# Turning a second x chunk on TensorE at the start of a gated attention and MLP kernel, and assigning the last tile's PSUM banks anew

## The chip, the cores and the metric

The kernel runs on one core of one Trainium2 chip. The metric is the device time of the program in microseconds (us). A "look" below is one profiled execution: its span (first to last instruction) is some 1.7 us shorter than the device time of the same run. All runs quoted here were fast: none lies more than 1.5% above the fastest of its kernel. Ratios are computed as the mean time of one kernel's fast runs over that of the other's fast runs of the same rounds, so they are not quite the ratio of the medians that are quoted.

Engines: PE is TensorE (PEld its weight loads), DVE is VectorE, ACT is ScalarE, POOL is GpSimd, SPq is the queue of SyncE, from which most DMAs are issued. A DMA "lands" at the last of its 16 landing records. "Granted clock" is the share of TensorE's full clock that the trace's clock records show; in these traces products of 128 columns follow each other by 107 ns at half clock and by 56 at full clock.

## The reference, cut to what matters

```python
def reference(A_x, A_wqkv, A_wo, B_x, B_w1, B_w2, B_w3, B_w4, gate_w):
    x = A_x                                                # 1 x 2048 x 640, bf16
    g = sigmoid((x * gate_w).sum(-1, keepdims=True))
    a = linear_attention(x, A_wqkv, A_wo)                  # needs q, k, v = x @ wqkv
    b = mixer_and_mlp(x, B_w1, B_w2, B_w3, B_w4)           # ends in x1 + gelu(ln(x1) @ w3) @ w4
    return g * a + (1 - g) * b
```

The kernel cuts the 2048 rows into 16 chunks of 128. Its first work is k = x @ wk for each chunk, with the gate as an extra, 641st column. For that, x must be transposed. Its last work is the product with W4, for four tiles of 512 rows each.

## The kernel before: the parts that matter

The head. Loads are issued on SPq and ACT's queue; chunk 0 of x is loaded plainly and transposed ("turned") on PE, chunks 1 to 15 are transposed by DMA. "Fillers" are products of constants that keep PE busy, meant to bring its full clock early (the clock records have it at 4.06 us here; the one look without fillers, below, at 7.58).

```python
    load_x(0, 1)                                           # SPq
    aq.dma_start(g5[:], gate_w...)                         # ACT's queue
    load_wk(sp, 1); load_wk(aq, 0); load_wk(aq, 2); load_wk(sp, 3); load_wk(aq, 4)   # 160 KB each
    for c0, c1 in ((1, 2), (2, 3), (3, 4), (4, 6), (6, 8), (8, 12), (12, 16)):
        load_xT(c0, c1)                                    # DMA transposes, SPq
    ...
    warmup(6)                                              # six fillers of 512 columns
    warmup(3, P)                                           # three of 128
    ... # turn x chunk 0 (bf16 transposes, two PSUM pairs), DVE copies it to xT;
    ... # the gate (5 rows) is transposed between the two groups
    warmup(3, P)
    for dc in range(DC):                                   # K of chunk 0, weight piece by piece
        k_mm(kp, 0, (dc,))
        if dc < DC - 1:
            warmup(1, 2 * P)
    k_evac(kp, 0)
    for c in range(1, NCH):
        pt = pair(); k_mm(pt, c, range(DC)); k_evac(pt, c)
```

The tail. A PSUM "pair" is two banks, and the kernel has four pairs. For the last tile, row blocks 1 and 3 are computed in the order wide group (512 columns), wide group, narrow group (128), narrow group; wide and narrow group of one block share one pair.

```python
    def w4_dst(t, cc, pts, hf):
        n = D - TS if t == NT - 1 and cc % 2 else LT
        return (pts[cc][:, 0, TS - n:TS], 0, n) if hf == 0 else (pts[cc][:, 1, 0:D - n], n, D)
    ...
        for cc, hf in ((1, 1), (3, 1), (1, 0), (3, 0)) if last else ((1, 0), (1, 1), (3, 0), (3, 1)):
            ...
            w4_mm(t, cc, pts, hf, False)
            if last:
                w4_part(t, cc, pts, hf)                    # DVE reads the group, DMA stores it
```

## Time and profile before

| what | before |
|---|---|
| device time | 265.14 us median of 3 runs; 265.31 of 4 with the run taken beside the changed kernel |
| span of the look | 263.5 us, PE busy 98% |
| turn of chunk 0 starts | 3.66 us |
| K of chunk 0 / 1 / 8 starts | 4.72 / 6.92 / 16.79 us |
| last product starts | 260.56 us |

The page's busy shares, and the engine line of the chain that ended last:

```profile
PE 258.4 (98%) x1722; PEld 161.0 (61%) x1740; DVE 141.4 (54%) x276; ACT 82.7 (31%) x123; POOL 20.2 (8%) x65
PE 92%; SPq 3%; DMA 3%; issue 1%; DVE 0%
```

With PE in 92% of the chain, only the places where PE waits can give time back. They are at the two ends. The timeline of PE in the head (start and duration in us, engine, line, operation, out<-in, shape, count, and in brackets the idle time and what ended it):

```profile
3.66 0.42 PE L205 MATMUL pp<-ident,x_sb 128*128 128x128 bf16 x2
4.01 0.18 PE L208 MATMUL pp<-ident,g 5*128 5x5 bf16 x1
...
4.72 0.43 PE L184 MATMUL pp<-wk_sb,xT 128*128 128x320 bf16 x2
...
5.83 0.43 PE L184 MATMUL pp<-wk_sb,xT 128*128 128x320 bf16 x2 [0.19 <-DMA wk_sb<-in_A_wqkv_dram]
...
6.59 0.64 PE L184 MATMUL pp<-wk_sb,xT 128*128 128x320 bf16 x3
```

PE turns x from 3.66 us, starts K at 4.72 and waits for the third weight piece, which landed at 5.79. Two of the three products in the last line end chunk 0; the third begins chunk 1, at 6.92, 0.05 us after the DMA transpose of chunk 1 landed at 6.87. Landings to the hundredth are read from the records in the trace; the view of a tile's instructions gives them as issue to landing, here for the transpose of chunk 1 (issued at 2.18):

```profile
L121 SPq DMA_TRANSPOSE xT<-in_A_x_dram x1: 1305/1305/1305, 2.2 to 2.2; - x1
...
DMA to landing us min/median/max: 4.7/4.7/4.7
```

From then on each chunk takes 1.362 us, until chunk 8 waits for the transpose of chunks 8 to 11 (PE timeline, later window):

```profile
16.79 11.07 PE L184 MATMUL pp<-wk_sb,xT 128*128 128x320 bf16 x80 [0.16 <-DMA xT<-in_A_x_dram]
```

In the tail, PE's weight loads and DVE show the other wait:

```profile
259.09 1.08 DVE L498 SCALAR_TENSOR_TENSOR oc<-pp,omg,x 128x512 bf16<-128x512 f32 x2 [2.05 <-PE pp L470]
259.87 1.66 SPq L500 DMA_DIRECT2D out_dram<-oc  x3
259.89 0.71 PEld L470 LDWEIGHTS <-h 128*128 128x128 bf16 x12 [0.24 <-issue]
260.81 0.35 DVE L498 SCALAR_TENSOR_TENSOR oc<-pp,omg,x 128x128 bf16<-128x128 f32 x1 [0.65 <-PE pp L470]
```

The last narrow group starts at 259.89 us, 336 ns after the product before it, where products of this size follow each other by 56 ns. It waits until DVE has read (259.09 to 259.84) the wide group of the same block, which lies in the other bank of the same pair. The view names no releaser for this gap ("issue"); that it is the read follows from the 0.05 us between the read's end and the start.

### The profile page before, as it was taken

The numbers are of one execution on the slowest core, as the hardware profiler recorded it, in microseconds if no ns is written. First come the engines' busy times: TensorE is split into PE (matmuls) and PEld (weight loads), VectorE is DVE, ScalarE is ACT, GpSimd is POOL, SyncE is SP. The second block draws the span as 40 slices with busy tenths as digits, with TensorE's granted clock in tenths as the row PEclk, the third lists the DMA queues.
The fourth block names the chain that finished last, engine by engine and source line by source line (L and its number), as shares of the span: only waits on it lengthen the run. The fifth ranks groups of instructions, "written<-read, shape, count | busy, mean of one in ns | idle before, by whom it ended". The sixth has DMA issues, their size and how long they took to land.

```text
span 263.5 us, 4244 instructions
## 1 busy us (share of the span) xinstructions
PE 258.4 (98%) x1722; PEld 161.0 (61%) x1740; DVE 141.4 (54%) x276; ACT 82.7 (31%) x123; POOL 20.2 (8%) x65
## 2 busy tenths in 40 slices
PE   8999999999999999999999999999999999999995
PEld 4767555688755644555667555667565577455743
DVE  1678778899947997955403464413356323112132
ACT  1555454321166236622502222412131332142100
POOL 5000050012210041001000001000001000000000
PEclk9999999999999999999999999999999999999999
DMA  7999988016672567700132000051100051100011
GB/s 191 175 193 370 374 261 322 0 27 124 124 99 57 101 111 172 248 0 2 25 75 77 25 0 2 0 100 52 50 0 2 0 101 52 50 0 2 0 50 50
DMA packets 46413, 24.14 MB, mean 92 GB/s; under 512 B 35770, under 2 KB 45626, under 8 KB 46394
## 3 DMA queue, kind: packets, MB, share of 16 engines
q1 hardware_dynamic: 45952, 23.39, 34.7%
q10 hardware_dynamic: 442, 0.49, 0.5%
q8 instruction: 13, 0.21, 0.3%
q14 instruction: 6, 0.05, 0.1%
HBM read 12.21 MB, written 2.62 MB: 56 GB/s over the span
## 4 chain that ended last, share of the span: by engine, by line
PE 92%; SPq 3%; DMA 3%; issue 1%; DVE 0%
PE pp L470 21%; PE pp L450 21%; PE pp L298 8%; PE pp L434 8%; PE pp L403 8%; PE pp L332 8%; PE pp L226 8%; PE pp L184 4%; DMA xT<-in_A_x_dram 3%; SPq L121 3%; PE pp L370 1%; PE pp L458 1%; PE pp L479 1%; PE pp L351 1%; PE pp L241 0%
## 5 line engine op out<-in xcount | busy, mean ns | idle before, releaser
L450 PE MATMUL pp<-lnxT,w_sb 128*128 128x512 bf16 x249 | 59.8, 379 | 0.6
L470 PE MATMUL pp<-w_sb,h 128*128 128x256 bf16 (+3 forms) x415 | 57.8, 299 | 0.3 <-issue 0.2
L452 ACT ACTIVATE h<-pp 128x1024 bf16<-128x1024 f32 (+1 forms) x28 | 26.9, 962 | 82.2 <-PE pp L450 82.2
L470 PEld LDWEIGHTS <-h 128*128 128x128 bf16 x416 | 39.3, 98 | 18.0 <-issue 1.3
L450 PEld LDWEIGHTS <-w_sb 128*128 128x128 bf16 x260 | 25.5, 98 | 26.8
L486 DVE SCALAR_TENSOR_TENSOR oc<-pp,omg,x 128x640 bf16<-128x640 f32 x14 | 12.0, 881 | 41.4 <-ACT h2x L461 21.3
L437 DVE SCALAR_TENSOR_TENSOR x<-pp,gate,x 128x640 f32<-128x640 f32 x16 | 13.9, 867 | 29.4 <-PE pp L434 29.4
L176 ACT ACTIVATE e<-pp 128x640 bf16<-128x640 f32 (+1 forms) x26 | 21.5, 827 | 9.5 <-PE pp L226 9.5
L434 PE MATMUL pp<-m_sb,pqT 128*128 128x320 bf16 x160 | 24.3, 299 | 0.0
L403 PE MATMUL pp<-w_sb,hsT 128*128 128x320 bf16 x160 | 23.9, 299 | 0.0
L406 DVE TENSOR_TENSOR x<-pp,x_sb 128x640 f32<-128x640 f32 x16 | 13.1, 820 | 19.7 <-PE pp L403 19.6
L184 PE MATMUL pp<-wk_sb,xT 128*128 128x320 bf16 (+1 forms) x160 | 22.7, 300 | 0.3 <-DMA wk_sb<-in_A_wqkv_dram 0.2
L298 PE MATMUL pp<-x_sb,pk 128*128 128x320 bf16 (+1 forms) x160 | 22.3, 300 | 0.0
L226 PE MATMUL pp<-xT,hsT 128*128 128x512 bf16 x98 | 21.6, 379 | 0.1
L298 PEld LDWEIGHTS <-pk 128*128 128x128 bf16 x160 | 18.8, 117 | 3.5
L403 PEld LDWEIGHTS <-hsT 128*128 128x128 bf16 x160 | 15.7, 98 | 8.2
L434 PEld LDWEIGHTS <-pqT 128*128 128x128 bf16 x160 | 15.7, 98 | 7.7
L184 PEld LDWEIGHTS <-xT 128*128 128x128 bf16 x160 | 15.4, 98 | 6.9 <-DMA xT<-in_A_x_dram 0.7
L332 PE MATMUL pp<-lnxT,w_sb 128*128 128x512 bf16 x76 | 17.9, 379 | 0.2
L226 PEld LDWEIGHTS <-hsT 128*128 128x128 bf16 x100 | 11.8, 118 | 9.7
L268 POOL TENSOR_SCALAR rstd<-mv 128x4 f32<-128x4 f32 (+1 forms) x11 | 3.4, 312 | 153.6 <-DVE mv L274 153.6
L177 DVE TENSOR_SCALAR e<-e 128x640 bf16<-128x640 bf16 (+1 forms) x26 | 9.5, 367 | 8.9 <-ACT e L176 7.5
(72 smaller groups left out, 195.0 us busy)
## 6 DMA issues: line engine op xcount, KB each, us to landing
out_dram<-oc SPq DMA_DIRECT2D x14, 160.0 KB, 1.8
w_sb<-in_B_w_dram SPq DMA_DIRECT2D x1, 2160.0 KB, 8.8
w_sb<-in_B_w_dram SPq DMA_DIRECT2D x1, 2080.0 KB, 10.0
x_sb<-in_A_x_dram SPq DMA_DIRECT2D x1, 1280.0 KB
x_sb<-in_A_x_dram SPq DMA_DIRECT2D x1, 1120.0 KB, 8.2
wo_sb<-in_A_wo_dram SPq DMA_DIRECT2D x6, 160.0 KB, 7.7
hsT<-in_A_wqkv_dram SPq DMA_DIRECT2D x1, 800.0 KB, 5.6
m_sb<-in_A_wqkv_dram SPq DMA_DIRECT2D x1, 800.0 KB, 12.8
```

Source lines behind the costliest of these rows:

```text
L176: nc.scalar.activation(ev, src, ACT.Exp)
L184: nc.tensor.matmul(pt[:, hf, 0:n], lhsT=xT[:, dc, c * P:(c + 1) * P], rhs=wk_sb[:, dc, hf * HD:hf * HD + n], start=(dc == 0), stop=(dc == ...
L226: nc.tensor.matmul(pt[:, t % 2, :], lhsT=wq_sb[:, dc, :].rearrange("p (m j) -> p j m", j=DC)[:, j], rhs=xT[:, dc, t * TS:(t + 1) * TS], st ...
L298: nc.tensor.matmul(pt[:, hf, 0:HD + hf], lhsT=w, rhs=x_sb[:, c, hf * HD:(hf + 1) * HD + hf], start=(c == 0), stop=(c == NCH - 1))
L332: nc.tensor.matmul(pt[:, i, :], lhsT=w, rhs=lnxT[t][:, dc, :], start=(dc == 0), stop=(dc == DC - 1))
L403: nc.tensor.matmul(pt[:, hf, 0:HD], lhsT=hsT[:, fc, 2 + c * P:2 + (c + 1) * P], rhs=w2_sb[:, fc, hf * HD:(hf + 1) * HD], start=(fc == 0), ...
L406: nc.vector.tensor_tensor(x1[:].rearrange("p (h e) -> p h e", h=2), pt[:, :, 0:HD], x_sb[:, c, 0:D].rearrange("p (h e) -> p h e", h=2), op ...
L434: nc.tensor.matmul(pt[:, hf, 0:HD], lhsT=pqT[:, j, c * P:(c + 1) * P], rhs=m_sb[:, j, hf * HD:(hf + 1) * HD], start=(j == 0), stop=(j == D ...
L437: nc.vector.scalar_tensor_tensor(x1, pt[:, :, 0:HD], gate[:, c:c + 1], x1, op0=ALU.mult, op1=ALU.add)
L450: nc.tensor.matmul(pt[:, k, :], lhsT=w3_sb[:, dc, fc * P:(fc + 1) * P], rhs=lnT[:, dc, :], start=(dc == 0), stop=(dc == DC - 1))
L452: nc.scalar.activation(h2[:, 2 * i * TS:(2 * i + n) * TS], pt[:].rearrange("p h e -> p (h e)")[:, 0:n * TS], ACT.Gelu_apprx_tanh)
L470: nc.tensor.matmul(dst, lhsT=st[t]["h2"][:, fc * TS + cc * P:fc * TS + (cc + 1) * P], rhs=w4_sb[:, fc, a:b], start=start and fc == 0, stop ...
```

## The change

Intent: in the head, start turning earlier, take the K pieces in the order in which they come, and take one transpose off the DMA queue by turning chunk 1 on PE too. In the tail, place the groups so that the last one does not wait for a read of its own pair. The core of the diff:

```diff
+    g5z = const.tile([P, P], BF16)                     # gate, padded with zeros to 128 rows
...
-    for c0, c1 in ((1, 2), (2, 3), (3, 4), (4, 6), (6, 8), (8, 12), (12, 16)):
+    load_x(1, 2)
+    for c0, c1 in ((2, 3), (3, 4), (4, 6), (6, 8), (8, 12), (12, 16)):
         load_xT(c0, c1)
...
-    warmup(6)
-    warmup(3, P)
+    warmup(5)
+    warmup(1, 3 * P)
...
+                if c:
+                    nc.tensor.transpose(dst, src, ident[:])          # chunk 1: bf16
+                else:
+                    nc.tensor.matmul(dst, lhsT=src, rhs=ident[:], start=True, stop=True)   # chunk 0: float32
+            if c == 0 and b == DC:
+                nc.tensor.matmul(pt[:, 1, 0:DC], lhsT=g5z[:], rhs=ident[:, 0:DC], start=True, stop=True)
...
+    turn(0)
+    warmup(1, TS)
+    for n, dc in enumerate((1, 0, 3, 2, 4)):
+        if n == DC - 1:
+            turn(1)
+        if n:
+            warmup(1, 2 * P)
+        k_mm(kp, 0, (dc,), ...)
...
+            homes = {0: (0, 1), 2: (1, 2)} if 0 in ccs else {1: (3, 3), 3: (2, 0)}   # last tile:
+            for cc, (w, n) in homes.items():                                          # pair of the wide,
+                wide, narrow = pts["pairs"][w][:, 0, :], pts["pairs"][n][:, 1, 0:NW]  # pair of the narrow group
```

The narrow group of block 3 thus lies in pair 0, its wide group in pair 2.

More of the change, by code (lines that the diff above doesn't have):

```diff
@@ L132 @@
     load_wk(aq, 4)
-    for c0, c1 in ((1, 2), (2, 3), (3, 4), (4, 6), (6, 8), (8, 12), (12, 16)):
+    load_x(1, 2)
+    for c0, c1 in ((2, 3), (3, 4), (4, 6), (6, 8), (8, 12), (12, 16)):
         load_xT(c0, c1)
     sp.dma_start(wq_sb, wqkv_v[:, :, 0:D])
-    load_x(1, 8)
+    load_x(2, 8)
     load_x(8, 16)
@@ L178, in phi, with k_mm @@
         nc.vector.scalar_tensor_tensor(dst, src, 0.0, ev, op0=ALU.max, op1=ALU.add)
-    def k_mm(pt, c, dcs, hfs=(0, 1), last=DC - 1):
+    def k_mm(pt, c, dcs, first=0, last=DC - 1):
         for dc in dcs:
-            for hf in hfs:
+            for hf in range(2):
                 n = HD + hf
                 nc.tensor.matmul(pt[:, hf, 0:n], lhsT=xT[:, dc, c * P:(c + 1) * P],
-                                 rhs=wk_sb[:, dc, hf * HD:hf * HD + n], start=(dc == 0), stop=(dc == last))
+                                 rhs=wk_sb[:, dc, hf * HD:hf * HD + n], start=(dc == first), stop=(dc == last))
     def k_evac(pt, c):
@@ L189, in k_evac @@
         phi(pk[:, c, :].rearrange("p (h e) -> p h e", h=2), pt[:, :, 0:HD], D)
+    k0_order = (1, 0, 3, 2, 4)
     warm = pair()
@@ L196, in warmup, with turn @@
             nc.tensor.matmul(warm[:, 1, 0:w], lhsT=one[:, 0:P], rhs=one[:, 0:w], start=True, stop=True)
-    warmup(6)
-    warmup(3, P)
+    nc.vector.memset(g5z[:], 0.0)
+    nc.vector.tensor_copy(g5z[0:DC, :], g5[:])
+    warmup(5)
+    warmup(1, 3 * P)
     kp = pair()
-    turns = [(pair()[:, 0, :].bitcast(BF16), a, b) for a, b in ((0, 2), (2, DC))]
-    tg = warm[:, 0, :].bitcast(BF16)
-    for n, (ptb, a, b) in enumerate(turns):
-        for dc in range(a, b):
-            nc.tensor.transpose(ptb[:, (dc - a) * P:(dc - a + 1) * P], x_sb[:, 0, dc * P:(dc + 1) * P], ident[:])
-        nc.vector.tensor_copy(xT[:, a:b, 0:P], ptb[:, 0:(b - a) * P].rearrange("p (c s) -> p c s", c=b - a))
-        if n == 0:
-            nc.tensor.transpose(tg[:, 0:DC], g5[:], ident[0:DC, 0:DC])
-            nc.vector.tensor_copy(wk_sb[:, :, D], tg[:, 0:DC])
-    warmup(3, P)
-    for dc in range(DC):
-        k_mm(kp, 0, (dc,))
-        if dc < DC - 1:
+    turns = [(pair(), a, b) for a, b in ((0, 2), (2, DC))]
+    def turn(c):
+        for pt, a, b in turns:
+            ptb = pt[:, 0, :].bitcast(BF16) if c else pt[:, 0, :]
+            for dc in range(a, b):
+                dst, src = ptb[:, (dc - a) * P:(dc - a + 1) * P], x_sb[:, c, dc * P:(dc + 1) * P]
+                if c:
[4 more added lines that the diff above has]
+                nc.tensor.matmul(pt[:, 1, 0:DC], lhsT=g5z[:], rhs=ident[:, 0:DC], start=True, stop=True)
+            nc.vector.tensor_copy(xT[:, a:b, c * P:(c + 1) * P],
+                                  ptb[:, 0:(b - a) * P].rearrange("p (c s) -> p c s", c=b - a))
+            if c == 0 and b == DC:
+                nc.vector.tensor_copy(wk_sb[:, :, D], pt[:, 1, 0:DC])
+    turn(0)
+    warmup(1, TS)
+    for n, dc in enumerate(k0_order):
+        if n == DC - 1:
+            turn(1)
+        if n:
             warmup(1, 2 * P)
+        k_mm(kp, 0, (dc,), first=k0_order[0], last=k0_order[-1])
     k_evac(kp, 0)
@@ L461, in w3_rest, with w4_tiles @@
         nc.scalar.activation(st[t]["h2x"][:], dst, ACT.Gelu_apprx_tanh)
-    def w4_dst(t, cc, pts, hf):
-        n = D - TS if t == NT - 1 and cc % 2 else LT
-        return (pts[cc][:, 0, TS - n:TS], 0, n) if hf == 0 else (pts[cc][:, 1, 0:D - n], n, D)
+    NW = D - TS
+    def w4_tiles(t, ccs, pts):
+        if t < NT - 1:
+            for cc in ccs:
+                pt = pair()
+                pts[cc, 0], pts[cc, 1] = (pt[:, 0, TS - LT:TS], 0, LT), (pt[:, 1, 0:D - LT], LT, D)
+                pts[cc, "rest"] = pt[:, 0, 0:LT]
+                pts[cc] = pt[:].rearrange("p h e -> p (h e)")[:, TS - LT:TS - LT + D]
+        else:
+            for _ in range(3 if 0 in ccs else 1):
+                pts["pairs"] = pts.get("pairs", []) + [pair()]
+            homes = {0: (0, 1), 2: (1, 2)} if 0 in ccs else {1: (3, 3), 3: (2, 0)}
+            for cc, (w, n) in homes.items():
+                wide, narrow = pts["pairs"][w][:, 0, :], pts["pairs"][n][:, 1, 0:NW]
+                pts[cc, 0], pts[cc, 1] = (narrow, 0, NW), (wide, NW, D)
     def w4_mm(t, cc, pts, hf, start):
-        dst, a, b = w4_dst(t, cc, pts, hf)
+        dst, a, b = pts[cc, hf]
         for fc in range(FF):
@@ L477, in w4_rest, with w4_stt @@
                     rows = slice(FR * v, FR * (v + 1))
-                    dst, a, b = w4_dst(t, u + 2 * v, pts, hf)
+                    dst, a, b = pts[u + 2 * v, hf]
                     nc.tensor.matmul(dst, lhsT=st[t]["h2x"][rows, u * P:(u + 1) * P],
                                      rhs=w4_sb[rows, FF, a:b], start=u == 1, stop=u == 0)
-    def w4_out(t, cc, pt):
+    def w4_stt(t, cc, oc, src, a, b):
         c = t * CPT + cc
-        x1 = st[t]["x1"][cc]
-        oc = outp.tile([P, D], BF16, name="oc")
-        nc.vector.scalar_tensor_tensor(oc[:], pt[:].rearrange("p h e -> p (h e)")[:, TS - LT:TS - LT + D],
-                                       omg[:, c:c + 1], x1[:], op0=ALU.mult, op1=ALU.add)
-        nc.sync.dma_start(out2[c * P:(c + 1) * P, :], oc[:])
@@ L490, with w4_store, w4_out @@
-    ocs = {}
-    def w4_part(t, cc, pts, hf):
-        c = t * CPT + cc
-        src, a, b = w4_dst(t, cc, pts, hf)
-        if cc not in ocs:
-            ocs[cc] = outp.tile([P, D], BF16, name="oc")
-        oc = ocs[cc]
         nc.vector.scalar_tensor_tensor(oc[:, a:b], src, omg[:, c:c + 1], st[t]["x1"][cc][:, a:b],
                                        op0=ALU.mult, op1=ALU.add)
+    def w4_store(t, cc, oc, a, b):
+        c = t * CPT + cc
         nc.sync.dma_start(out2[c * P:(c + 1) * P, a:b], oc[:, a:b])
+    def w4_out(t, cc, pts):
+        oc = outp.tile([P, D], BF16, name="oc")
+        if t < NT - 1:
+            w4_stt(t, cc, oc, pts[cc], 0, D)
+        else:
+            for hf in range(2):
+                w4_stt(t, cc, oc, *pts[cc, hf])
+        w4_store(t, cc, oc, 0, D)
@@ L502, in w4_tile @@
     def w4_tile(t):
-        pts = {cc: pair() for cc in (0, 2)}
+        last = t == NT - 1
+        pts = {}
+        w4_tiles(t, (0, 2), pts)
         for cc in (0, 2):
-            if t + 1 < NT:
+            if not last:
                 x1_scale(t + 1, cc)
-            for hf in range(2):
+            for hf in (1, 0):
                 w4_mm(t, cc, pts, hf, True)
-        for cc in (1, 3):
-            pts[cc] = pair()
+        w4_tiles(t, (1, 3), pts)
         w4_rest(t, pts)
-        if t + 1 < NT:
-            w3_rest(t + 1, pts[0][:, 0, 0:LT])
+        if not last:
+            w3_rest(t + 1, pts[0, "rest"])
@@ L514, in w4_tile @@
         for cc in (0, 2):
-            w4_out(t, cc, pts[cc])
-        last = t == NT - 1
+            w4_out(t, cc, pts)
+        ocs = {}
         for cc, hf in ((1, 1), (3, 1), (1, 0), (3, 0)) if last else ((1, 0), (1, 1), (3, 0), (3, 1)):
-            if t + 1 < NT and hf == 0:
+            if not last and hf == 0:
                 x1_scale(t + 1, cc)
@@ L521, in w4_tile @@
             if last:
-                w4_part(t, cc, pts, hf)
+                if hf == 1:
+                    ocs[cc] = outp.tile([P, D], BF16, name="oc")
+                w4_stt(t, cc, ocs[cc], *pts[cc, hf])
+                w4_store(t, cc, ocs[cc], *pts[cc, hf][1:])
             elif hf == 1:
-                w4_out(t, cc, pts[cc])
+                w4_out(t, cc, pts)
     for cc in range(CPT):
```

## The prediction

> **What bounds it.** The page's busy shares: PE 98% of a 263.5 us span, DVE 54%, ACT 31%. The chain of waits is PE 92%. Only PE's idle time can be won, at the two ends.
>
> Head (timeline of 0 to 28 us):
> - fillers (six of 512 columns, three of 128) run at half clock, 427 and 107 ns apart, from 0.83 us; the turn of chunk 0 starts at 3.66, though x chunk 0 landed at about 3.1;
> - the 5-row gate transpose costs two gaps of about 0.2 us; K of chunk 0 starts at 4.72;
> - the third weight chunk lands at 5.8: PE waits 0.36 us; chunk 1 starts at 6.92, as its DMA transpose lands;
> - then 1.362 us per chunk, until chunk 8 waits 0.33 us for its DMA transpose and starts at 16.79. From there the chain is PE to the end.
>
> Tail (timeline of 252 to 263.5 us): the last 128-column group starts at 259.89 instead of 259.61: it waits for DVE's read (259.09 to 259.84) of the other bank of the same pair, 0.28 us.
>
> **What the change does.**
> 1. 2944 filler columns instead of 3456: the turn starts at about 3.23 (-0.43). [...]
> 2. Float32 products: DVE's copies get dearer. Bf16 copies took 0.29 us (256) and 0.36 (384), 0.52 ns per element; float32 reads from PSUM take 1.04 (512 in 0.75 us, 128 in 0.35). Estimate: 0.43 and 0.56 us. [...] The gate column's copy now comes last, at about 4.80, and the first 321-column K product needs it: K starts in earnest at about 4.85, not 4.72. The early turn is given back.
> 3. Order 1, 0, 3, 2, 4 meets the weights as they land (chunk 3 about 5.6, 2 about 5.8): the 0.36 us wait shrinks to about 0.15.
> 4. Turning chunk 1 adds five products (0.28 us) before the last K piece. x chunk 1 should land at about 6.2, just in time. Chunk 1 starts at about 7.0: 0.1 us LATER than before.
> 5. The SyncE queue swaps a 1.3 us transpose issue for a 0.4 us load, so later transposes come 0.9 us earlier. Chunk 8's lands at about 15.9 instead of 16.7, and PE, there at 7.0 + 7 x 1.362 = 16.55, does not wait: 16.79 becomes 16.55, -0.24 us.
> 6. Tail: the last narrow group lies in a pair that DVE left long before: the 0.28 us wait goes. Columns and stores stay. Blocks 0 and 2 need two DVE reads (0.35 + 0.75 against 0.84), off the chain.
>
> The middle has the same instructions: nothing.
>
> Clock: [...] products are 107 ns apart at 3.7 us, 56 at 4.2. [...] I expect the same.
>
> **Prediction:** 265.14 - 0.24 - 0.28 = 264.6 us; 264.1 to 265.2 holds it 8 times in 10. Faster by over 2%: 0.01; within: 0.98; slower: 0.01.
>
> **To check:** turn at 3.2; first K pair split by a wait until about 4.85; chunk 1 at 7.0; chunk 8 without a wait at 16.5; last narrow group 56 ns after the previous one; last product near 260.0 (span 263.0).
>
> **Wrong if:** x chunk 1 lands well after 6.3 (up to +0.5); [...] transposes do not come earlier; or another wait takes the freed time.

Passages on the hardware that no trace of this case showed are cut from this text, and the cuts are marked: a reason for the dearer float32 copies, the reason for padding the gate, a rule for the clock, and one risk (a later full clock). Of the two gaps put down to the five-row transpose, the first lies directly before it (it starts 243 ns after the product before, at 4.01 us), the second before the fillers that come later (301 ns, at 4.55). For the 6.2 us of step 4 no working is given.

## The result

| | before | changed |
|---|---|---|
| device time, median of 4 runs | 265.31 us (265.03 to 265.60) | 265.05 us (264.83 to 265.26) |
| ratio of means | | 0.9990 (0.9973 to 1.0007) |
| turn of chunk 0 starts | 3.66 us | 3.24 us |
| K of chunk 0 / 1 / 8 starts | 4.72 / 6.92 / 16.79 us | 4.52 / 7.46 / 17.01 us |
| last product starts | 260.56 us | 260.49 us |
| span of the look | 263.5 us | 263.4 us |

The time is within the predicted range, but the two terms of the sum are not what was predicted: in this look the head loses 0.22 us (predicted: a gain of 0.24), and the tail gains the predicted 0.28. The page of the changed kernel:

```profile
PE 258.0 (98%) x1721; PEld 160.0 (61%) x1740; DVE 142.7 (54%) x282; ACT 82.7 (31%) x123; POOL 20.1 (8%) x65
PE 96%; DMA 2%; issue 1%; SPq 0%; DVE 0%
```

PE in the head:

```profile
3.24 0.73 PE L216 MATMUL pp<-ident,x_sb 128*128 128x128 bf16 x5
3.77 0.20 PE L218 MATMUL pp<-ident,g5z 128*128 128x5 bf16 x1
...
4.52 0.50 PE L186 MATMUL pp<-wk_sb,xT 128*128 128x320 bf16 x2 [0.31 <-DMA wk_sb<-in_A_wqkv_dram]
...
5.88 0.43 PE L186 MATMUL pp<-wk_sb,xT 128*128 128x320 bf16 x2 [0.37 <-DMA wk_sb<-in_A_wqkv_dram]
...
6.79 0.45 PE L214 MATMUL pp<-ident,x_sb 128*128 128x128 bf16 x5
...
7.19 0.58 PE L186 MATMUL pp<-wk_sb,xT 128*128 128x320 bf16 x3
```

The turn comes 0.42 us earlier, but then PE waits for weights at 4.52 and 5.88, and for x chunk 1 at 6.79. Only then come the turn of chunk 1, a filler and the last K piece of chunk 0, and chunk 1 starts at 7.46. DVE's copies in between (the first line is both copies of the turned chunk 0, the second the gate column):

```profile
3.69 0.89 DVE L219 CAST xT<-pp 128x256 bf16<-128x256 f32 x2 [1.27 <-PE pp L216]
4.50 0.17 DVE L222 CAST wk_sb<-pp 128x5 bf16<-128x5 f32 x1
```

The plain load of x chunk 1, issued at 2.18 like the transpose before, needed 4.6 us (it landed at 6.74, the transpose before at 6.87):

```profile
L119 SPq DMA_DIRECT2D x_sb<-in_A_x_dram x1: 434/434/434, 2.2 to 2.2; - x1
...
DMA to landing us min/median/max: 4.6/4.6/4.6
```

Chunk 8 no longer waits (one run of 96 products without an idle mark), but PE comes to it later:

```profile
14.83 13.24 PE L186 MATMUL pp<-wk_sb,xT 128*128 128x320 bf16 x96
```

And the tail:

```profile
258.88 1.65 PEld L500 LDWEIGHTS <-h 128*128 128x128 bf16 x26
259.30 1.08 DVE L514 SCALAR_TENSOR_TENSOR oc<-pp,omg,x 128x512 bf16<-128x512 f32 x2 [2.05 <-PE pp L500]
...
260.75 0.35 DVE L514 SCALAR_TENSOR_TENSOR oc<-pp,omg,x 128x128 bf16<-128x128 f32 x1 [0.38 <-PE pp L500]
```

All 26 narrow weight loads now run through without a gap.

### The profile page after: what moved, and what is told of

Same layout as the page of the kernel before. It is cut to its first block, busy times and chain, and to the rows that moved or that the text cites. A ratio compares the mean times of both kernels' runs of the same rounds, so it can differ in the third digit from the quotient of the medians.

```text
span 263.4 us, 4250 instructions
## 1 busy us (share of the span) xinstructions
PE 258.0 (98%) x1721; PEld 160.0 (61%) x1740; DVE 142.7 (54%) x282; ACT 82.7 (31%) x123; POOL 20.1 (8%) x65
## 4 chain that ended last, share of the span: by engine, by line
PE 96%; DMA 2%; issue 1%; SPq 0%; DVE 0%
PE pp L500 22%; PE pp L467 21%; PE pp L315 8%; PE pp L451 8%; PE pp L420 8%; PE pp L349 8%; PE pp L243 8%; PE pp L186 8%; DMA x_sb<-in_A_x_dram 2%; PE pp L387 1%; PE pp L475 1%; PE pp L509 1%; PE pp L368 1%; PE pp L258 0%; SPq L125 0%
## 5 line engine op out<-in xcount | busy, mean ns | idle before, releaser
L500 PE MATMUL pp<-w_sb,h 128*128 128x384 bf16 (+3 forms) x414 | 57.6, 299 | 0.2 <-issue 0.2
L500 PEld LDWEIGHTS <-h 128*128 128x128 bf16 x416 | 38.3, 98 | 19.3 <-issue 1.1
L514 DVE SCALAR_TENSOR_TENSOR oc<-pp,omg,x 128x640 bf16<-128x640 f32 (+2 forms) x20 | 14.4, 748 | 45.1 <-ACT h2x L478 21.3
L180 DVE SCALAR_TENSOR_TENSOR pk<-pp,e 128x640 bf16<-128x640 f32 x16 | 13.2, 825 | 1.7
```

The source lines that it names most:

```text
L500: nc.tensor.matmul(dst, lhsT=st[t]["h2"][:, fc * TS + cc * P:fc * TS + (cc + 1) * P], rhs=w4_sb[:, fc, a:b], start=start and fc == 0, stop ...
L514: nc.vector.scalar_tensor_tensor(oc[:, a:b], src, omg[:, c:c + 1], st[t]["x1"][cc][:, a:b], op0=ALU.mult, op1=ALU.add)
```

## The experiments

The first rival theories were these. LOADS: x chunk 1's plain load shares the DMA engines with the last K weight pieces (in the look of the changed kernel the mean busy share of the 16 engines is 0.99 from 2.20 to 5.30 us), so that it and they land late, and the turn then lies in the chain. COPIES, or PE WORK: the float32 copies and the turn's own products hold the head. CHANCE: the late landings of the one look were scatter. All experiments were timed in 5 rounds against the kernel before; those of one group ran in the same rounds on one chip.

### Group 1: the parts of the change

**Tail alone** (head of before, last tile of after):

```diff
 # the kernel before, with w4_tiles, w4_mm, w4_rest, w4_stt, w4_store, w4_out, w4_tile of the changed one
```

> The head of before with the last tile of after. Every theory: chunk 8 of K still starts at about 16.8 us, the last narrow group follows the one before it by 56 ns instead of 336 ns, and the time falls by about 0.28 us (265.3 to 265.0). If the tail's gain were given back by the split stores or by the queue, the time would stay at that of before.

Measured: 264.79 us median (264.69 to 265.43, 5 runs), ratio 0.9994 (0.9982 to 1.0006). Chunk 8 started at 16.68 and the last product at 260.16 us. The distance between the two is 243.48 us, against 243.77 before.

**Head alone** (head of after, last tile of before):

```diff
 # the changed kernel, with w4_dst, w4_mm, w4_rest, w4_out, w4_part, w4_tile of the one before
```

> The head of after with the last tile of before, which keeps its 0.28 us wait. Theory LOADS (x chunk 1's plain load shares the DMA engines with the last pieces of the K weights, so these and x itself land late): fifth weight piece at about 6.9 instead of 6.3, chunk 1 of K at about 7.4 instead of 6.92, chunk 8 at about 17.0 without a wait, time about 0.2 us above before. Theory CHANCE (the late landings of the one profile were scatter): chunk 1 at about 7.0 in this second look, chunk 8 at 16.55, time 0.2 us below before.

Measured: 266.05 us median (265.05 to 267.87, 6 runs), ratio 1.0038 (1.0010 to 1.0067): three runs near 265.3, and 266.47, 266.60 and 267.87. Neither theory had foreseen runs that long. The look fell on the longest of them. PE in its head:

```profile
5.24 0.27 PE L199 MATMUL pp<-const-bfloat16-1.0 128*128 128x256 bf16 x1
6.94 0.48 PE L186 MATMUL pp<-wk_sb,xT 128*128 128x320 bf16 x2 [1.43 <-DMA wk_sb<-in_A_wqkv_dram]
...
7.96 0.74 PE L214 MATMUL pp<-ident,x_sb 128*128 128x128 bf16 x5
```

and three stretches of it in the view by windows (window, length, busy time and count of PE, PEld, DVE, ACT and POOL, granted PE clock, DMA share, GB/s):

```profile
3.80:7.20 3.40, 1.73 (x12) 0.87 (x11) 0.87 (x3) 0.22 (x1) 0.84 (x3) 1.00 1.24 218
7.20:10.60 3.40, 3.40 (x19) 2.17 (x17) 0.96 (x3) 0.77 (x2) 0.00 (x0) 0.50 1.00 195
10.60:14.00 3.40, 3.40 (x26) 2.45 (x25) 2.31 (x5) 1.53 (x4) 0.00 (x0) 1.00 1.12 193
```

The weight piece that K uses third came only at 6.90 us and x chunk 1 at 7.76. The lateness is that of a few landings: 14 of the 16 landings of that weight piece were in by 5.22, and 12 of the 16 of x chunk 1 by 5.68. PE had been busy for 1.73 of 3.40 us, with one gap of 1.43, and the clock went back to half for the next 3.4 us: the clock records change at 3.79, 7.20 and 10.61 us, 3.41 apart. A pair of K products took 0.74 us in the slow stretch (from 7.43), and takes 0.43 at full clock (in the changed kernel's look, from 5.88). That PE's idle time brought this about is the author's estimate from this one look; in the look of the split version below PE sat idle for 1.01 us before 6.66, and a pair of K products still took 0.43 us after it.

**Chunk 1 by DMA transpose again** (all else of after):

```diff
-    load_x(1, 2)
-    for c0, c1 in ((2, 3), ...
+    for c0, c1 in ((1, 2), (2, 3), ...
...
-        if n == DC - 1:
-            turn(1)
```

> After, but chunk 1 of x comes by DMA transpose as before and is not turned on PE; the float32 products for chunk 0, the order 1,0,3,2,4, the fillers and the new tail stay. Theory LOADS: the fifth weight piece lands at about 6.3 again, K of chunk 0 is done by about 6.7, chunk 1 starts when its transpose lands, near 6.9, and chunk 8 waits for its transpose until about 16.8: time 0.28 us below before, 0.2 below after. Theory COPIES (step 2 of the prediction: float32 copies and the gate column that comes last hold the head): chunk 0's K still ends as late as in after (about 7.4) and the time stays at that of after.

Measured: 265.04 us median (264.62 to 265.23), ratio 0.9996 (0.9983 to 1.0009). No run was long, in the rounds in which the head alone had three of six. The fifth weight piece landed at 6.51; chunk 1 started at 7.39 rather than 6.9. These are the numbers that COPIES expected (about 7.4, and the time of the changed kernel), but the look shows other causes: the full clock came only at 6.79 us, so that the K pieces ran at half speed, and the transpose of chunk 1 landed at 7.10, so that 6.9 was out of reach. The run does not decide between the two theories; the second look of the changed kernel below, with the same copies and chunk 1 at 6.83, speaks against COPIES.

**Chunks 8 to 11 in two transposes** (tail alone, plus):

```diff
-    for c0, c1 in (..., (6, 8), (8, 12), (12, 16)):
+    for c0, c1 in (..., (6, 8), (8, 10), (10, 12), (12, 16)):
```

> The head of before and the new tail, with the DMA transpose of chunks 8 to 11 cut in two (8 and 9, 10 and 11). If chunk 8's wait is only for the landing of a needlessly large transpose, it goes: chunk 8 starts at about 16.45 instead of 16.8, time about 0.6 us below before (0.28 from the tail, 0.33 from the wait). If smaller transposes cost the queue as much as they save, or a later chunk waits instead, the time is that of the tail change alone, 0.28 below before.

Measured: 265.21 us median (264.41 to 265.47, 6 runs), ratio 0.9999 (0.9986 to 1.0012): a miss. The transpose of chunks 8 and 9 did land early, at 14.13. But in this look the weight piece needed third came at 6.62, chunk 1 started at 7.70, and chunk 8 at 17.24 without a wait. In the look of the tail alone, too, chunk 8 did not wait at all (its transpose landed at 16.14, PE came at 16.68). The look of before is the only one of all 14 that has this wait. It takes two things: PE at chunk 8 early, and a late landing. Before had PE there at about 16.45 (6.92 + 7 x 1.362) and the landing at 16.74; in the four other looks with the same loads it landed at 15.56 to 16.32. The wait is chance as much as structure.

### Group 2: the load of chunk 1

The unchanged new kernel once more, on another chip:

> The changed kernel once more, to tell a rule from scatter, since the first looks show landings of the K weights that differ by up to 1 us between runs of one head. Theory LOADS: x chunk 1 lands no earlier than its DMA transpose did (6.6 to 7.6 in the looks at the old head), and chunk 1 of K starts about 0.7 us after that landing (five turns, filler, last K piece) against 0.05 us in the old head; time within 0.1 us of before. Theory CHANCE: with an ordinary landing (about 6.2) chunk 1 starts at 7.0 and the time is 264.6.

Measured: 265.16 us median (264.50 to 265.32, 5 runs), ratio 0.9992 (0.9979 to 1.0006). The look was a run of 264.50 us, and in it x chunk 1 landed at 6.11:

```profile
5.72 0.44 PE L186 MATMUL pp<-wk_sb,xT 128*128 128x320 bf16 x2
6.16 0.45 PE L214 MATMUL pp<-ident,x_sb 128*128 128x128 bf16 x5
...
6.56 1.13 PE L186 MATMUL pp<-wk_sb,xT 128*128 128x320 bf16 x7
```

The turn waited 0.16 us at most (the K products before it are 136 ns apart, the last of them started at 5.86), chunk 1 started at 6.83, chunk 8 at 16.38 without a wait. This is the head that had been predicted (7.0 and 16.55). But the look fell on one of the two short runs of five (264.50 and 264.53; the others 265.16 to 265.32), and the median is that of before in these rounds (265.13), as LOADS expected. CHANCE holds for the size of the landing; the 0.72 us from landing to chunk 1 are the same as in the first look (6.74 to 7.46).

**No load for chunk 1** (its turn takes chunk 0 again). Its output is wrong, which doesn't matter for the time.

```diff
-    load_x(1, 2)
...
-    x_sb[:, c, dc * P:(dc + 1) * P]
+    x_sb[:, 0, dc * P:(dc + 1) * P]
...                                                    # the later load of x takes chunk 1 too
```

> After, but the turn of chunk 1 takes x chunk 0 again, so that neither a plain load nor a transpose of chunk 1 is in the queue at this place (K of chunk 1 is wrong on purpose). All products, copies and fillers stay. Theory LOADS: turn and last K piece wait only for the fifth weight piece, which lands at 6.1 to 6.5; chunk 1 starts at about 6.8 instead of 7.46, and the time falls by about 0.6 us against after (to about 264.4). Theory PE WORK (the turn's own products and the float32 copies cost the head): chunk 1 still starts at about 7.3 and the time stays at that of after.

Measured: 264.69 us median (264.40 to 265.47, 6 runs), ratio 0.9989 (0.9975 to 1.0003); chunk 1 at 6.91. That is not 0.6 us below the new kernel of the same rounds but 0.1 (means 264.85 and 264.94), which these runs do not resolve. In the one look at the new kernel in these rounds the loads were early, and there was little to take away. PE ran from the second K piece to chunk 1 without a pause, so 6.91 is what its own work gives here, with the full clock from 5.27 us.

**The load doubled** (chunks 1 and 2, 320 KB):

```diff
-    load_x(1, 2)
+    load_x(1, 3)
...                                                    # the later load of x starts at chunk 3
```

> After, with the suspected cost doubled: the plain load before the transposes takes x chunks 1 and 2 (320 KB; chunk 2 is still transposed by DMA too). Theory LOADS: the landing that the turn waits for comes about 0.45 us later (about 7.2) and chunk 1 starts at about 7.9; time about 0.4 us above after. Theory PE WORK: no change.

Measured: 265.84 us median (265.35 to 265.98, 5 runs), ratio 1.0023 (1.0010 to 1.0036), a mean of 265.76 against 264.94 for the new kernel in the same rounds: 0.8 us more, twice what was expected. The load landed at 7.46, the fifth weight piece at 7.48, chunk 1 started at 8.18: again landing plus 0.72, with PE waiting for the load:

```profile
7.51 0.45 PE L214 MATMUL pp<-ident,x_sb 128*128 128x128 bf16 x5 [0.47 <-DMA x_sb<-in_A_x_dram]
...
7.91 1.26 PE L186 MATMUL pp<-wk_sb,xT 128*128 128x320 bf16 x8
```

PE WORK, which expected no change, falls.

**Two chunks at once** (chunks 0 and 1 loaded first and turned, each weight piece used for both; old fillers before the turn, none between pieces; transposes of 8 to 11 in two; new tail):

```diff
     load_x(0, 1)
+    load_x(1, 2)
...
+    turn(0); warmup(3, P); turn(1)
+    for dc in range(DC):
+        for c in range(2):
+            k_mm((kp, warm)[c], c, (dc,))
```

> An attempt at a better head: bf16 turns as before, x chunks 0 and 1 loaded plainly FIRST, both turned, and each weight piece used for both chunks as it lands (no fillers between), the transpose of chunks 8 to 11 cut in two, the new tail. Theory LOADS: the weight pieces all land about 0.4 us later (the fifth at about 6.9), but when it is in, two chunks are done 0.54 us later: chunk 2 starts at about 7.5 instead of 8.3, chunk 8 at about 15.7; time about 0.8 us below the tail change alone, 264.1. Theory PE WORK: the extra turn holds the head and chunk 2 starts no earlier than 8.2.

Measured: 264.97 us median (264.25 to 265.63, 6 runs), ratio 0.9994 (0.9979 to 1.0009): no better than the tail alone. In the look some landings were late (of 16 landings for weight piece 3, 12 were in by 5.72, the last three came at 7.47 to 7.50), but PE did not wait for them. K started at 5.36, its first four products ran at half speed, the full clock came only at 6.78, and the one wait, for the second piece used (landed at 6.63), was some 0.25 us; from there PE ran without a pause to chunk 2 at 8.89. So its own work held this head, as PE WORK expected (8.2 or later), at half clock to begin with.

### Group 3: old and new head side by side

The tail alone and the new kernel in the same rounds, on a further chip:

> The old head with the new tail, again, beside the changed kernel on the same chip. Theory NO GAIN IN THE HEAD (x chunk 1 loaded plainly lands when its transpose did, and what the later transposes gain is lost by the turn): mean within 0.15 us of the changed kernel's, about 0.25 us below before. Theory HEAD PAYS: the changed kernel's mean is 0.2 us or more below this one's. Theory HEAD COSTS: 0.2 us or more above.

> The changed kernel a third time, in the same rounds as the tail alone. Both looks so far agree that chunk 1 of K starts 0.72 us after x chunk 1's landing, which was 6.11 in one and 6.74 in the other: expected here chunk 1 at landing + 0.72, a landing between 6.1 and 7.8, no wait before chunk 8, and a time between 264.5 and 265.5 that follows the landing.

Measured: tail alone 264.88 us median (264.37 to 264.93, 5 runs), ratio 0.9981 (0.9969 to 0.9993). In the look of the tail alone the narrow groups again run without a gap (PE, which has the last 26 products in one line):

```profile
258.82 1.61 PE L483 MATMUL pp<-w_sb,h 128*128 128x128 bf16 x26
```

New kernel 265.87 us median (264.96 to 267.73, 6 runs: 264.96, 265.18, 265.76, 265.98, 266.22, 267.73), ratio 1.0029 (1.0004 to 1.0055). HEAD COSTS, here by 1.3 us in the mean. The one of 267.73 had a mean granted clock of 0.994, as the long run of the head alone. The look was a short run: x chunk 1 landed at 6.20, but chunk 1 of K started 1.08 us later, not 0.72, since the K pieces ran at half speed until 5.9 us (products of 320 columns 270 ns apart instead of 136).

**Two chunks, with fillers** (the two-chunk version above with the changed kernel's fillers; shortened):

```diff
+    warmup(5); warmup(1, 3 * P); ...; turn(0); warmup(1, TS, kp); turn(1)     # bf16 turns, padded gate
     for dc in range(DC):
         for c in range(2):
             k_mm(kps[c], c, (dc,))
+        if dc < DC - 1:
+            warmup(1, 2 * P, turns[0][0])
```

> A second attempt at a better head: as the two-chunk head, but with the short start fillers and the zero-padded gate product of after, bf16 turns, and a 256-column filler after each weight piece, which were missing. Theory CLOCK [...]: the full clock comes at 3.6 to 5.3 us more often, chunk 2 starts at about 7.5 when the fifth piece lands at 6.8, mean about 264.3. Theory LANDINGS ONLY: the mean stays at the first attempt's 265.0, because the last weight piece sets the end of the head whatever PE does.

CLOCK is here the theory that the half clock until 6.78 us in the first attempt's look, and one late piece, cost the gain, and that the fillers end it sooner.

Measured: 264.83 us median (264.74 to 265.32, 5 runs), ratio 0.9990 (0.9977 to 1.0003). In the look the fifth piece landed at 6.51, but PE worked without a pause from 4.75 us, at half speed until 5.8, and reached chunk 2 only at 8.44. It was now limited by its own products and fillers. CLOCK's numbers (7.5 and 264.3) did not come true. The mean, 264.92, is near the 265.0 of LANDINGS ONLY, but not for its reason, since PE was still at work for almost two microseconds after the last piece had landed.

### Group 4: no fillers at all

```diff
-    warmup(6)
-    warmup(3, P)
...
-    warmup(3, P)
     for dc in range(DC):
         k_mm(kp, 0, (dc,))
-        if dc < DC - 1:
-            warmup(1, 2 * P)
```

> The old head with the new tail, without any filler products (none before the turn, none between the K pieces), so that PE idles while it waits for loads. It tests what the slow runs of the new head (266 to 267.9, the one profiled lost the full clock from 7.20 to 10.61 us after idling from 5.35 to 6.94) have to do with idle time. Theory CLOCK [...]: full clock only at 7 to 10.5 us in every run, K products 270 ns apart until then, time 1 to 2.5 us above the tail alone (about 266 to 267.5). Theory LANDINGS ONLY: the loads set the head, fillers do nothing, chunk 1 starts near 6.9 and the time stays at about 264.9.

CLOCK is here the theory, put to the test, that without fillers the full clock comes late.

Measured: 265.69 us median (265.11 to 266.16, 6 runs), ratio 1.0021 (1.0004 to 1.0037): three runs near 265.2 and three near 266.14. In the look, one of the short runs, the full clock came at 7.58 us, as expected; but with the weights early (the fifth at 6.15) chunk 1 still started at 7.28. The fillers are worth something, about half of what was expected and not in every run: the mean is 0.2% above that of before, where the tail alone was 0.1 to 0.2% below it, though in other rounds.

### All looks together

Landings of x chunk 1 and of the fifth weight piece, and starts of K of chunks 1 and 8, in us:

| look | chunk 1 of x | lands | fifth piece | chunk 1 | chunk 8 | chunk 8 to last product |
|---|---|---|---|---|---|---|
| before | DMA transpose | 6.87 | 6.35 | 6.92 | 16.79 | 243.77 |
| tail alone, first | DMA transpose | 6.64 | 6.06 | 7.14 | 16.68 | 243.48 |
| tail alone, second | DMA transpose | 7.14 | 6.56 | 7.19 | 16.73 | 243.48 |
| 8 to 11 in two | DMA transpose | 7.64 | 7.04 | 7.70 | 17.24 | 243.48 |
| after, first | plain, turned | 6.74 | 6.92 | 7.46 | 17.01 | 243.48 |
| after, second | plain, turned | 6.11 | 6.29 | 6.83 | 16.38 | 243.48 |
| after, third | plain, turned | 6.20 | 6.42 | 7.28 | 16.82 | 243.48 |
| head alone | plain, turned | 7.76 | 7.97 | 9.25 | 19.46 | 243.76 |
| chunk 1 by transpose again | DMA transpose | 7.10 | 6.51 | 7.39 | 16.93 | 243.48 |
| no fillers | DMA transpose | 6.73 | 6.15 | 7.28 | 16.97 | 243.48 |
| no load for chunk 1 | none, turned | - | 5.96 | 6.91 | 16.46 | 243.48 |
| load doubled | plain, turned | 7.46 | 7.48 | 8.18 | 17.73 | 243.48 |

The two looks at two-chunk heads are left out, since their heads are built differently.

The last column settles the tail: in all twelve looks with the new last tile, those two included, the stretch is 243.48 us, in the two with the old one 243.76 and 243.77. Nothing in between depends on the head. So every difference but these 0.28 to 0.29 us is made before chunk 8.

## Why the prediction was right and wrong

The number was right (265.05 in 264.1 to 265.2), one term of its sum (the tail) was right, and the other (the head) was not a number that one look can give. There was luck in it: the range also held "no change" (265.14), and the same kernel had a median of 265.87, outside the range, in its third set of rounds.

1. *Turn at 3.23:* right, 3.24. With the padded gate (and float32 products in place of the transposes) the gap before the gate is gone: the products follow each other by 107 ns (x at 3.67, gate at 3.77), where the five-row product had come 243 ns after the one before it.
2. *Float32 copies:* right, they were dearer. The two copies took 0.89 us together (0.99 estimated, 0.65 as bf16 copies before), and the first 321-column product waited for the gate column until 4.72 (4.85 predicted). In the first look it did not decide anything, because PE then waited for weights longer than that.
3. *The wait for weights shrinks to 0.15:* wrong in the first look, where piece 3 came at 5.84 rather than 5.6 and PE's third pair of K products started 0.54 us later than without a wait; right in the second look, where there was none (third pair at 5.34).
4. *x chunk 1 at 6.2, chunk 1 of K at 7.0:* this is the step that failed, with step 5. I took a landing as a number read once, and it is a draw: the four looks at the new head had 6.11, 6.20, 6.74 and 7.76. The prediction named a late landing as its first risk, but for at most 0.5 us. What is fixed is what follows it. The old head started chunk 1 0.05 us after the landing whenever the landing came last (before, tail alone second, 8 to 11 in two: 0.05, 0.05, 0.06). The new head needs at least 0.72 us: five turns, a filler and the last K piece all stand behind that wait. And the plain load came within the same range as the transpose that it replaced (6.64 to 7.64 in six looks), at the same place in the same queue, behind the same weights; one that comes early gains little, since the turn follows. The loads of the two queues came late together: the fifth piece, issued from ACT's queue, landed 0.18 to 0.22 us after x chunk 1 in all four looks, early or late. What ties them is not shown. Doubling the load fits (7.46 and 7.48 against 6.11 and 6.29 in the same rounds), but the look of the head alone was as late without it; there the times decide (0.8 us in the mean).
5. *Later transposes 0.9 us earlier, no wait at chunk 8:* half right. The transpose of chunks 8 to 11 was issued earlier (8.56 to 8.72 in the three looks of the changed kernel, 9.31 to 9.51 with the old loads), and no look of the new head waits there. But its landing is a draw too: 15.51 to 16.42 with the new head, 15.56 to 16.74 with the old loads. Of these the look of before had the latest, and it alone has the wait. So I counted as a gain of the change a wait that the one look of before happened to have; the two looks at the same head with the new tail have none.
6. *Tail, 0.28 us:* right in all looks (0.28 to 0.29).

*A later full clock* was named as a risk, with the judgment that the changed kernel would be the same as before. That judgment was wrong. Of 21 runs with the new head (after three times, head alone), seven took 265.7 us or more and two of them 267.7 or more; of the 48 runs of the kernel before in these rounds none took over 265.60, and of the 16 with the old head and the new tail (with and without the split) none over 265.47. The look at one such run shows, in this order: late weights, PE idle for 1.43 us, half clock from 7.20 to 10.61 us. No look fell on the five runs between 265.7 and 266.6, but their granted clocks are 1.000 three times and 0.999 twice, where the two runs that took 267.7 or more have 0.994. So the two with 0.999 did not lose such a stretch in mid-run (3.41 us at half clock are 0.006 of the span); of the other three this is less sure, since a look without any clock record (the third at the changed kernel) reads 1.000 too. A full clock that first comes late stays possible: the look without fillers had it at 7.58 us and still reads 1.000. Late landings alone would do: an estimate from the second look (264.50 us with the landing at 6.11), with 0.28 taken off the head alone for its old tail, puts the five at landings of about 7.4 to 7.9, and 7.76 was seen. None of this is shown. The part of x chunk 1's load in the long runs was only argued as well: for it speaks that the version without this load had none in the rounds where the head alone had three of six, and that with the load doubled four of five runs took 265.8 or more where the changed kernel had none.

The best supported version is the tail alone: 0.9994 (0.9982 to 1.0006) and 0.9981 (0.9969 to 0.9993) of before on two chips. Only on the second is the gain resolved by the times; there it is also clear of the changed kernel (1.0029). What stays open is why the new head cost nothing in two sets of rounds and about 1 us in two others. That the landings scatter is seen (x chunk 1 from 6.11 to 7.76 us), as is that the full clock does (first at 3.83, 5.27 and 6.79 us in three looks with the same fillers up to the turn); and that of a late load a few of the 16 landings can come late (in the first look of the changed kernel 13 of x chunk 1 by 5.81 us, the last three at 6.72 to 6.74); but not what sets this.

## What to carry to other kernels

Before moving work from a DMA to an engine, ask when the data lands and what will stand behind that landing: here a load in the same place of the queue landed in the same range (6.11 to 7.76 us against 6.64 to 7.64), and the turn was then added to the chain. The microseconds at the start of this kernel are draws from the landings of the first loads and from when the full clock comes (3.83 to 7.58 us in the looks named), so read several looks and not one, and judge a head by its spread. A wait between two engines inside one kernel, such as a PSUM pair shared by a read and a write, was the opposite here: it was worth 0.28 to 0.29 us in every look and could be predicted from one.
